# Batch 1's first transform stage cut into half steps between batch 0's column pairs, early weight decoding from one ring of buffers, twelve weight bands decoded ahead of the feed-forward part

## The chip, the cores and the metric

The kernel runs on one core of a Trainium2 chip. The metric is the device time of one launch in microseconds. Before the change the median of three runs is 2731.85 us (2729.75 to 2733.45).

## The reference

Eight batches of 3008 tokens of 256 channels go through a frequency-domain mixing and then through a gated feed-forward part; both weight matrices of the latter come in float64, and the kernel decodes them itself into two float32r words each (hi and lo).

```
X = rfft(x, axis=1);  Xr, Xi = real, imag            # x: 8 x 3008 x 256
Yr = Xr @ w_r - Xi @ w_i + b_r
Yi = Xr @ w_i + Xi @ w_r + b_i
Y  = soft_threshold(Yr, 0.01) + 1j * soft_threshold(Yi, 0.01)
y  = irfft(Y, n=3008, axis=1).reshape(24064, 256)
h  = y @ w_in                                        # w_in: 256 x 2048, float64
out = (h * clip(h + 3, 0, 6) / 6) @ w_out            # w_out: 2048 x 256, float64
```

## The kernel before

**The transform of a batch** has three parts, each a Python generator whose yields are the points at which other work may be put between its steps. `stage1(b)` (line 252) takes seven sets of rows of x; for each set it forms a sum `e` and a difference (in place in `xin`), and for each of the two (the index c) splits it into hi and lo (`xs`: a ScalarE cast and a subtraction), multiplies by the 47-point transform (three matmuls into `ps_a`), copies the product to `a` and stores it to the DRAM scratch scr1. That is fourteen steps, one yield each. For batch 0 the work is spread over VectorE and GpSimd and all inputs are loaded at once; for later batches every sum, difference and subtraction is GpSimd's, `xin`, `e`, `xs` and `a` have one buffer each, and the next set is loaded behind the second product of a set.

`middle(b)` (line 339) handles 24 columns in twelve pairs. A pair is loaded from scr1 (`bt`, with its matrix `f`), transformed (`s2`, four matmuls of line 362, split into `X`), mixed with the weights, biased and thresholded (`s3`, tile `tc`), moved across partitions by four DMAs (`zt`), split again (`s4`, tile `z`), transformed back (`s5`), copied to `pt` and stored to the DRAM scratch scr2. `segment(b, k)` (line 454) loads columns of scr2 (`qt`), runs the last 47-point transform (line 482) and adds and subtracts the halves into `raw`, the feed-forward part's input. `prepare(c)` (line 521) forms the Strassen-like differences `T` of a chunk of 512 tokens and splits them into seven `yb` operands on GpSimd.

**Decoding.** `decode` (line 169) loads a band of float64 words (`st`) and rebuilds exponent and mantissa in seven VectorE instructions (lines 184 to 192) and two ScalarE ones. `in_band` then runs six GpSimd instructions and three hi/lo splits whose subtractions are VectorE's; `out_band` runs two GpSimd multiplications. There are eight bands of each matrix. `EARLY` and `LATE` name the tiles that lend their space to `st`, `e` and `m`, `r`.

**The feed-forward part** walks over 376 units: 47 chunks of 512 tokens by 8 bands. A unit's phases a to d are seven blocks of three matmuls each into `pd`, `pb` and `pc` (with the band's `w_in`), its gate is one ScalarE activation, one VectorE multiplication and a split into `gs`, and three units later four blocks of three matmuls go into `po` (with the band's `w_out`). The first chunk needs band f at its f-th unit, so all sixteen bands must be there when the first eight units are through; the end of that pass is the first `ot` (line 604), where a chunk's `po` is scaled and sent out.

**What sets the order.** Up to the feed-forward part it is the code of lines 610 to 622: a decode, then 36 steps of batch 0's `middle` with a decode behind every fifth, then six steps of batch 1's `stage1`, then two segments of batch 0 and the first chunk's operands. Eight bands are decoded by then. From there on, `lay` (line 627) spreads generators over numbered slots, four to a unit; the rest of batch 1's `stage1` goes over the units 1 to 8, batch 1's `middle` begins at unit 9, and the other eight bands are decoded behind the units 2 to 6 (line 697). Each engine works its instructions off in order, and so does the queue of SyncE (SP), which issues every DMA; a scheduler may move an instruction of one engine past its neighbours, so the final order stands in the built program.

## Time and profile before

| | |
|---|---|
| median of three runs | 2731.85 us |
| the profiled execution | 2734.95 us |
| its span, first to last instruction | 2733.1 us |
| busy: PE, DVE, ACT, POOL | 95%, 73%, 67%, 31% of the span |
| mean granted TensorE clock | 0.976 |

The share of PE is an average: in the page's forty slices of 68.3 us PE stands at five or six tenths in the first four and at nine from the seventh on. The chain of work that ended last is PE for 68% of the span. Times below count from the first instruction of the span.

### The profile page before, as it was taken

To read this page: it belongs to the slowest core of one execution; us is meant where nothing else is said; L and a number is where in the kernel's file an instruction comes from. 1 tells how busy PE (TensorE), PEld (TensorE's weight loads), DVE (VectorE), ACT (ScalarE), POOL (GpSimd) and SP (SyncE) were. 2 spreads that over 40 slices of the span, in tenths; PEclk is the share of its full clock that TensorE was granted. 3 is DMA by queue.
4 is the path that set the end of the run, shared out by engine and by line. 5 is a ranking of instruction groups with operands and counts; after the bars stand their busy time and mean duration, and the time that the engine had idled before them with its cause. 6 is when DMAs were issued, how large, how long until landed. Compare 5 with 4: busy or idle time off the path is not lost.

```text
span 2733.1 us, 44514 instructions
## 1 busy us (share of the span) xinstructions
PE 2593.4 (95%) x16432; PEld 2317.1 (85%) x16432; DVE 1983.8 (73%) x3222; ACT 1832.4 (67%) x3591; POOL 836.6 (31%) x788
## 2 busy tenths in 40 slices
PE   5656999999999999999999999999999999999999
PEld 4544888888898898888898888988898999999997
DVE  7627877777777777777777777777777777766666
ACT  4434667766776676677767677767676667666766
POOL 3356433333322233223422343233221212122210
PEclk9876999999999999999999999999999999999999
DMA  6532442232222222222312232123221121100000
GB/s 193 159 90 68 117 123 82 82 82 80 65 68 81 74 82 67 68 75 73 90 57 72 75 96 68 57 74 95 74 67 56 58 61 49 49 23 31 16 19 16
DMA packets 150818, 200.51 MB, mean 73 GB/s; under 512 B 16975, under 2 KB 104775, under 8 KB 150599
## 3 DMA queue, kind: packets, MB, share of 16 engines
q1 hardware_dynamic: 150599, 197.65, 25.0%
q8 instruction: 129, 2.11, 0.3%
q14 instruction: 90, 0.74, 0.1%
HBM read 97.45 MB, written 74.97 MB: 63 GB/s over the span
## 4 chain that ended last, share of the span: by engine, by line
PE 68%; DVE 11%; ACT 8%; issue 6%; POOL 5%; DMA 2%; ACTq 0%; DVEq 0%; SPq 0%; POOLq 0%
PE po L136 29%; PE pb L136 15%; PE ps_a L136 9%; PE pc L136 8%; PE pd L136 4%; ACT r L581 3%; DVE r L583 3%; PE ps_a L482 2%; DVE gs L130 2%; ACT gs L129 2%; PE ps_a L362 2%; DMA xin<-in_x 2%; DVE h L546 2%; DVE X L130 1%; POOL xs L130 1%
## 5 line engine op out<-in xcount | busy, mean ns | idle before, releaser
L136 PE MATMUL po<-gs,w_out_hi 128*128 128x512 f32 x3008 | 954.3, 398 | 3.4 <-DVE gs L130 3.4
L583 DVE SCALAR_TENSOR_TENSOR r<-r,h 128x1024 f32<-128x1024 f32 x376 | 478.5, 1273 | 386.6 <-ACT r L581 386.6
L136 PEld LDWEIGHTS po<-gs,w_out_hi 128*128 128x128 f32 x3008 | 567.6, 189 | 76.3 <-DVE gs L130 4.7
L136 PE MATMUL po<-gs,w_out_lo 128*128 128x512 f32 x1504 | 609.7, 406 | 6.8 <-POOL w_out_lo L227 5.3
L136 PE MATMUL pb<-yb,w_in_hi 128*128 128x256 f32 x3008 | 604.5, 282 | 0.8 <-POOL yb L130 0.8
L130 DVE TENSOR_TENSOR gs<-r,gs 128x1024 fp32r<-128x1024 f32 x376 | 474.6, 1262 | 120.7 <-ACT gs L129 117.4
L581 ACT ACTIVATE r<-h,three 128x1024 f32<-128x1024 f32 x376 | 433.2, 1152 | 186.2 <-DVE h L546 183.6
L136 PEld LDWEIGHTS pb<-yb,w_in_hi 128*128 128x128 f32 x3008 | 465.9, 190 | 51.4 <-POOL yb L130 1.2
L129 ACT CAST gs<-r 128x1024 fp32r<-128x1024 f32 x376 | 396.0, 1053 | 130.9 <-DVE r L583 116.2
L130 POOL TENSOR_TENSOR yb<-T,yb 128x256 fp32r<-128x256 f32 x188 | 205.9, 1106 | 826.4 <-ACT yb L129 826.1
L136 PE MATMUL pb<-yb,w_in_lo 128*128 128x256 f32 x1504 | 428.1, 285 | 8.7 <-ACT p L543 4.0
L546 DVE TENSOR_TENSOR h<-pc,u 128x256 f32<-128x256 f32 x752 | 313.5, 417 | 77.7 <-PE pc L136 66.0
L543 ACT COPY u<-pb 128x256 f32<-128x256 f32 x752 | 277.4, 371 | 112.4 <-PE pb L136 106.1
L136 PEld LDWEIGHTS pb<-yb,w_in_lo 128*128 128x128 f32 x1504 | 285.6, 190 | 68.2 <-ACT p L543 8.0
L136 PE MATMUL pc<-yb,w_in_hi 128*128 128x256 f32 x1504 | 299.4, 280 | 0.5 <-POOL yb L130 0.5
L136 PEld LDWEIGHTS po<-gs,w_out_lo 128*128 128x128 f32 x1504 | 285.1, 190 | 16.6 <-POOL w_out_lo L227 5.9
L574 ACT COPY h<-pb 128x256 f32<-128x256 f32 x376 | 140.4, 373 | 142.6 <-PE pb L136 141.1
L136 PE MATMUL pc<-yb,w_in_lo 128*128 128x256 f32 x752 | 217.0, 289 | 18.3 <-DVE h L546 17.4
L136 PEld LDWEIGHTS pc<-yb,w_in_hi 128*128 128x128 f32 x1504 | 231.4, 189 | 1.6 <-POOL yb L130 0.7
L130 POOL TENSOR_TENSOR xs<-xin,xs 120x512 fp32r<-120x512 f32 (+1 forms) x52 | 69.8, 1343 | 343.1 <-ACT xs L129 293.4
L136 PEld LDWEIGHTS pc<-yb,w_in_lo 128*128 128x128 f32 x752 | 142.4, 189 | 32.9 <-DVE h L546 31.0
L546 DVE TENSOR_TENSOR h<-pd,p 128x256 f32<-128x256 f32 x376 | 156.4, 416 | 3.5 <-ACT p L543 3.0
(128 smaller groups left out, 4015.7 us busy)
## 6 DMA issues: line engine op xcount, KB each, us to landing
bt<-scr SPq DMA_DIRECT2D x96, 256.0 KB, 3.0
zt<-tc SPq DMA_DIRECT2D x384, 64.0 KB, 2.0
scr<-pt SPq DMA_DIRECT2D x96, 256.0 KB, 2.0
out<-ot SPq DMA_DIRECT2D x94, 256.0 KB, 2.0
xin<-in_x SPq DMA_DIRECT2D x48, 480.0 KB, 4.7
scr<-a SPq DMA_DIRECT2D x96, 240.0 KB, 2.5
qt<-scr SPq DMA_DIRECT2D x96, 240.0 KB, 3.4
f<-in_f SPq DMA_DIRECT2D x96, 128.0 KB, 2.9
```

The costliest lines, as they stand in the source:

```text
L129: nc.scalar.copy(out=hi, in_=src)
L130: (on or nc.vector).tensor_tensor(out=lo, in0=src, in1=hi.bitcast(F32), op=ALU.subtract)
L136: nc.tensor.matmul(out=ps, lhsT=a, rhs=b, start=start and n == 0, stop=stop and n == len(todo) - 1, skip_group_check=more,)
L362: nc.tensor.matmul(out=psv[:, dh, :, u, :], lhsT=data[:, u, dh * P : (dh + 1) * P], rhs=f[:, u, :], start=True, stop=True,)
L482: nc.tensor.matmul(out=ps[:, cs * w + g * rows : cs * w + (g + 1) * rows], lhsT=qt[:rows, cs, g, dh * P : (dh + 1) * P], rhs=f47_s[2][:row ...
L543: nc.scalar.copy(out=t, in_=ps)
L546: nc.vector.tensor_tensor(out=hs[i][:, u, half * H : (half + 1) * H], in0=ps, in1=keep.pop((i, n)), op=ALU.add)
L574: nc.scalar.copy(out=hs[i][:, 1, :H], in_=pb)
L581: nc.scalar.activation(out=r, in_=h, func=AF.Relu, bias=three, scale=1.0)
L583: nc.vector.scalar_tensor_tensor(out=r, in0=r, scalar=6.0, in1=h, op0=ALU.min, op1=ALU.mult)
```

## The change

`stage1` of the batches 1 to 7 gets a second yield per product, between the split of its operand and the matmuls, so it has 28 steps of half the size. From the eleventh of the 36 steps of batch 0's `middle`, every second one is followed by such a half step (13 in all). In front of each of the first two segments stand two decodes with the `LATE` tiles and two more half steps. So twelve bands are decoded and seventeen half steps done (eight and a half products) where there were eight bands and six products; the other eleven half steps go over the units 2 to 8, and four bands stay for the units 4 to 6.

`EARLY` now takes `e`, `m` and `r` from the nine `yb` buffers alone; the four words of `w_four` move from there to `T` and `qt`. `LATE` uses tiles of `middle` (`X`, `bt`, `tc`, `z`, `zt`, `pt`) instead of those of `stage1`, and batch 0's `pt` uses `ot` instead of `xs` and `xin`. From batch 2 on `stage1` is laid with 29 calls over the same units where it had 15.

```diff
@@ -226,8 +226,8 @@
         for t, part in zip(wout_s, (mf, rf)):
             nc.gpsimd.tensor_tensor(out=cut(t, 1), in0=part, in1=base, op=ALU.mult)
 
-    EARLY = (("raw", "yb", "yb", "yb"), ("raw", "ot", "T"), ("raw", "ot", "qt"))
-    LATE = (("xin", "bt", "tc"), ("X", "e", "xs"))
+    EARLY = (("raw", "yb", "yb", "yb"),)
+    LATE = (("X", "bt", "tc"), ("z", "bt", "zt", "pt"))
     bands = [(in_band, 0), (in_band, 1)]
     for f in range(nf):
         bands.append((out_band, f))
@@ -280,6 +280,8 @@
                 tag = ("xs", "z", "h")[q % 3 if b == 0 else 0]
                 xs = [t[:rows, :w] for t in twin([P, 2 * D], F32R, "xs", tag)]
                 split(*xs, src, nc.vector if b == 0 and (c == 0 or i % 2 == 0) else nc.gpsimd)
+                if b:
+                    yield
                 ps = room(b == 0 and c)
                 product(ps[:rows, :w], [([t[:rows, c * R47 : c * R47 + rows] for t in f47_s[:2]], xs)])
                 a = space([P, 2 * D], F32, "a", ("a", "h", "h")[q % 3] if b == 0 else "a")[:rows, :w]
@@ -324,7 +326,7 @@
             nc.sync.dma_start(out=bias_s, in_=bias)
             nc.sync.dma_start(out=sgn_s, in_=sgn)
             g64_t = loaded(g64, P, P, "g64", "ot")
-            w_four += [[space([P, 2 * D], F32R, "w", "yb") for _ in range(2)] for _ in range(2)]
+            w_four += [twin([P, 2 * D], F32R, "w", tag) for tag in ("T", "qt")]
             todo = weights()
         if i >= 8:
             next(todo, None)
@@ -428,7 +430,7 @@
         def s5(g):
             ps = room(b == 0)
             product(ps, [(g64_s, [t.rearrange("p k d -> p (k d)") for t in zs.pop(g)])])
-            pt = space([P, 2, D], F32, "pt", tag(g, "pt", "xs", "xin"))
+            pt = space([P, 2, D], F32, "pt", tag(g, "pt", "ot", "ot"))
             nc.scalar.copy(out=pt, in_=ps.rearrange("p (k d) -> p k d", d=D))
             nc.sync.dma_start(out=dst[:, 2 * g : 2 * g + 2, :], in_=pt)
 
@@ -607,17 +609,21 @@
             nc.sync.dma_start(out=out[dh * P : (dh + 1) * P, c * T : (c + 1) * T], in_=ot)
 
 
-    mid, nxt = middle(0), stage1(1)
+    mid, nxt, early = middle(0), stage1(1), 0
     decode_next(EARLY)
     for i in range(3 * (NK // 2)):
         next(mid)
         if i % 5 == 3:
             decode_next(EARLY)
+        if i >= 10 and i % 2 == 0:
+            early += 1
+            next(nxt)
     run(mid)
-    early = 6
-    for i in range(early):
-        next(nxt)
     for k in range(2):
+        for _ in range(2):
+            decode_next(LATE)
+            early += 1
+            next(nxt)
         run(segment(0, k))
     run(prepare(0))
 
@@ -647,8 +653,7 @@
         g = prepare(c)
         for n in range(8):
             slots.setdefault(max(0, 4 * (8 * c - 5) + 2 * n), []).append(g)
-    rest = 14 - early
-    lay(nxt, rest + 1, 1, 8)
+    lay(nxt, 29 - early, 2, 8)
     for b in range(B):
         for k in range(len(SEGS)):
             if (b, k) not in ((0, 0), (0, 1)):
@@ -656,7 +661,7 @@
         if b:
             lay(middle(b), 3 * (NK // 2) + 2, max(9, per * (b - 1) - 14), begin[b, 0] - 1.5)
         if b > 1:
-            lay(stage1(b), 15, max(9, per * (b - 2) - 10), per * (b - 1) - 16)
+            lay(stage1(b), 29, max(9, per * (b - 2) - 10), per * (b - 1) - 16)
 
     def fill(q):
         for g in slots.get(q, []):
```

What the new code does to the order is seen in three places. First PE, from the last column pairs of batch 0 to its first segment (`xs` products are batch 1's stage 1, `z` products the pairs' back transform, `qt` products the segments). Before, with the last two pairs and the two products of the first set just ahead of these rows:

```order
L136 MATMUL ps_a<-xs,f_lo 120x512
L136 MATMUL ps_a<-xs,f_hi 120x512 x2
L136 MATMUL ps_a<-xs,f_lo 120x512
L136 MATMUL ps_a<-xs,f_hi 120x512 x2
L136 MATMUL ps_a<-xs,f_lo 120x512
L136 MATMUL ps_a<-xs,f_hi 120x512 x2
L136 MATMUL ps_a<-xs,f_lo 120x512
L482 MATMUL ps_a<-f_all,qt 128x120
L136 MATMUL ps_a<-xs,f_hi 120x512 x2
L482 MATMUL ps_a<-f_all,qt 128x120 x7
L136 MATMUL pd<-yb,w_in_lo 128x256
```

and with the change:

```order
L136 MATMUL pb<-z,g_lo 128x512
L136 MATMUL pb<-z,g_hi 128x512 x2
L136 MATMUL ps_a<-xs,f_lo 120x512
L136 MATMUL ps_a<-xs,f_hi 120x512 x2
L136 MATMUL pb<-z,g_lo 128x512
L136 MATMUL pb<-z,g_hi 128x512 x2
L136 MATMUL pb<-z,g_lo 128x512
L136 MATMUL pb<-z,g_hi 128x512 x2
L484 MATMUL ps_a<-f_all,qt 128x120 x8
L136 MATMUL ps_a<-xs,f_lo 120x512
L136 MATMUL ps_a<-xs,f_hi 120x512 x2
L484 MATMUL ps_a<-f_all,qt 128x120 x8
```

Before, all six products stand between the last pair and the first segment. With the change the products stand between the pairs, and only one, behind the first segment, is left in that place.

Second DVE, from the last pair's `z` on (`raw` is written by the segments, `h` is the feed-forward part's). Before:

```order
L130 TENSOR_TENSOR w_in_lo<-m,w_in_hi 128x256
L130 TENSOR_TENSOR w_in_lo<-m,w_in_hi 128x128
L130 TENSOR_TENSOR w_in_lo<-e,w_in_hi 128x512
L130 TENSOR_TENSOR z<-zt,z 128x512
L492 TENSOR_TENSOR raw<-ps_a,odd 128x240
L504 TENSOR_TENSOR raw<-ps_a,odd 128x230
L492 TENSOR_TENSOR raw<-ps_a,odd 128x240
L504 TENSOR_TENSOR raw<-ps_a,odd 128x230
L492 TENSOR_TENSOR raw<-ps_a,odd 128x42
L492 TENSOR_TENSOR raw<-ps_a,odd 128x198
L504 TENSOR_TENSOR raw<-ps_a,odd 128x230
```

and with the change, where the last `z` is 16 rows above the first of these:

```order
L191 TENSOR_SCALAR m<-st 128x512
L187 SCALAR_TENSOR_TENSOR e<-st,e 128x512
L192 SCALAR_TENSOR_TENSOR m<-st,m 128x512
L184 TENSOR_SCALAR e<-st 128x512
L189 TENSOR_SCALAR m<-st 128x512
L185 TENSOR_SCALAR e<-e 128x512
L191 TENSOR_SCALAR r<-st 128x512
L186 TENSOR_SCALAR e<-e 128x512
L192 SCALAR_TENSOR_TENSOR r<-st,r 128x512
L494 TENSOR_TENSOR raw<-ps_a,odd 128x240
L506 TENSOR_TENSOR raw<-ps_a,odd 128x230
L187 SCALAR_TENSOR_TENSOR e<-st,e 128x512
```

Between the last `z` and the first `raw` there was nothing; now the end of one `w_out` band, all of a `w_in` band and a `w_out` band, and six of the seven decoding instructions of a further `w_in` band stand there, 24 rows.

Third DVE in the first pass of the feed-forward part. Before, about the fifth unit's gate:

```order
L184 TENSOR_SCALAR e<-st 128x512
L189 TENSOR_SCALAR m<-st 128x512
L185 TENSOR_SCALAR e<-e 128x512
L191 TENSOR_SCALAR m<-st 128x512
L186 TENSOR_SCALAR e<-e 128x512
L192 SCALAR_TENSOR_TENSOR m<-st,m 128x512
L187 SCALAR_TENSOR_TENSOR e<-st,e 128x512
L130 TENSOR_TENSOR w_in_lo<-m,w_in_hi 128x256
L130 TENSOR_TENSOR gs<-r,gs 128x1024
L130 TENSOR_TENSOR w_in_lo<-m,w_in_hi 128x128
L130 TENSOR_TENSOR w_in_lo<-e,w_in_hi 128x512
```

and with the change, about the gate of the second unit:

```order
L130 TENSOR_TENSOR gs<-r,gs 128x1024
L548 TENSOR_TENSOR h<-pd,p_1562 128x256
L585 SCALAR_TENSOR_TENSOR r<-r,h 128x1024
L548 TENSOR_TENSOR h<-pc,u_1594 128x256
L130 TENSOR_TENSOR w_in_lo<-m,w_in_hi 128x256
L130 TENSOR_TENSOR w_in_lo<-m,w_in_hi 128x128
L130 TENSOR_TENSOR w_in_lo<-e,w_in_hi 128x512
L548 TENSOR_TENSOR h<-pc,u_1538 128x256
L130 TENSOR_TENSOR gs<-r,gs 128x1024
L191 TENSOR_SCALAR m<-st 128x512
L585 SCALAR_TENSOR_TENSOR r<-r,h 128x1024
```

Before, three `w_in` bands have their `w_in_lo` subtractions in such a place, ahead of or between the gates; with the change one band has, and it is these rows.

## Rows read from the trace of the kernel before

**Rows 1.** Busy time of each engine by stage; the clock is the granted TensorE clock.
```profile
core 0: us, PE busy (x) PEld busy (x) DVE busy (x) ACT busy (x) POOL busy (x), PEclk, DMA share, GB/s
40.00:128.00 88.00, 63.37 (x419) 57.12 (x420) 68.17 (x124) 39.81 (x77) 30.40 (x34) 0.87 0.54 160
128.00:172.00 44.00, 15.65 (x41) 8.60 (x40) 1.43 (x4) 8.50 (x18) 17.86 (x17) 0.54 0.35 94
172.00:200.00 28.00, 22.05 (x122) 18.82 (x122) 13.87 (x29) 15.47 (x35) 18.65 (x21) 0.89 0.36 92
200.00:298.00 98.00, 67.13 (x305) 55.35 (x304) 71.17 (x113) 47.77 (x97) 60.09 (x52) 0.74 0.30 82
300.00:400.00 100.00, 98.02 (x643) 88.77 (x644) 79.77 (x124) 70.15 (x140) 34.49 (x28) 1.00 0.42 119
```

**Rows 2.** PE's waits between 128 and 172 us: total, times, longest.
```profile
PE ps_a L136 <- ACT xs L129: 20.2, 6, 6.8
```

**Rows 3.** Timeline of POOL, batch 1's stage 1: start, duration, instruction, idle before.
```profile
142.97 1.26 POOL L276 TENSOR_TENSOR e<-xin 120x512 f32<-120x512 f32 x1 [4.13 <-DMA xin<-in_x]
149.32 1.27 POOL L130 TENSOR_TENSOR xs<-xin,xs 120x512 fp32r<-120x512 f32 x1 [2.52 <-ACT xs L129]
154.72 1.26 POOL L276 TENSOR_TENSOR e<-xin 120x512 f32<-120x512 f32 x1 [4.13 <-DMA xin<-in_x]
```

**Rows 4.** Timeline of SP, the first segment's load.
```profile
131.90 0.89 SPq L463 DMA_DIRECT2D qt<-scr  x2
```

**Rows 5.** Timeline of DVE, from the last pair to the second segment.
```profile
126.80 0.69 DVE L130 TENSOR_TENSOR z<-zt,z 128x512 fp32r<-128x512 f32 x1
165.28 0.41 DVE L492 TENSOR_TENSOR raw<-ps_a,odd 128x240 f32<-128x240 f32 x1 [37.80 <-ACT odd L490]
177.34 0.39 DVE L504 TENSOR_TENSOR raw<-ps_a,odd 128x230 f32<-128x230 f32 x1
```

**Rows 6.** DVE between 40 and 128 us, line 411, by lines: count, busy, mean ns.
```profile
L411 DVE TENSOR_SCALAR tc<-tc 128x512 f32<-128x512 f32 x12 | 7.9, 657 | 0.1
```

**Rows 7.** Timeline of DVE, line 411 once with POOL idle.
```profile
116.52 0.41 DVE L411 TENSOR_SCALAR tc<-tc 128x512 f32<-128x512 f32 x1
```

**Rows 8.** Timeline of DVE and POOL, one early w_in band from start to end.
```profile
95.64 0.43 DVE L184 TENSOR_SCALAR e<-st 128x512 int32<-128x512 int32 x1 [2.54 <-DMA st<-in_w_in]
97.93 0.68 DVE L187 SCALAR_TENSOR_TENSOR e<-st,e 128x512 int32<-128x512 int32 x1
...
98.75 1.27 POOL L203 TENSOR_TENSOR m<-m 128x512 f32<-128x512 f32 x1 [13.17 <-ACT m L193]
103.48 0.52 POOL L213 TENSOR_TENSOR e<-m,e 128x128 f32<-128x128 f32 x1
...
104.68 0.69 DVE L130 TENSOR_TENSOR w_in_lo<-e,w_in_hi 128x512 fp32r<-128x512 f32 x1 [1.00 <-ACT w_in_hi L129]
```

**Rows 9.** Timeline of POOL, the first chunk's operands.
```profile
177.30 0.74 POOL L526 TENSOR_TENSOR T<-raw,T 128x256 f32<-128x256 f32 x1 [0.60 <-DVE raw L492]
182.12 0.73 POOL L130 TENSOR_TENSOR yb<-raw,yb 128x256 fp32r<-128x256 f32 x1
```

**Rows 10.** PE's waits between 200 and 290 us.
```profile
PE pd L136 <- DVE w_in_lo L130: 8.4, 2, 5.3
PE po L136 <- POOL w_out_lo L227: 5.3, 2, 3.5
```

**Rows 11.** DVE's waits between 200 and 300 us.
```profile
DVE h L546 <- PE pc L136: 12.1, 6, 5.6
DVE w_in_lo L130 <- ACT w_in_hi L129: 7.1, 4, 2.9
```

**Rows 12.** Timeline of DVE, the first finished chunk.
```profile
298.37 0.69 DVE L604 TENSOR_SCALAR ot<-po 128x512 f32<-128x512 f32 x1
```

**Rows 13.** The chain that ended last, three pieces: start, length, what.
```profile
291.82 0.35 PE pb L136 x3
292.54 0.70 PE po L136 x3
293.35 1.44 PE ps_a L136 x12
```

**Rows 14.** PE's stage 1 products, second and third matmul, by lines: busy, mean, idle before.
```profile
L136 PE MATMUL ps_a<-xs,f_hi 120*120 120x512 f32 (+1 forms) x210 | 69.6, 413 | 11.1 <-POOL xs L130 9.8 <-DVE xs L130 1.2
```

**Rows 15.** PE's waits between 128 and 300 us.
```profile
PE ps_a L136 <- POOL xs L130: 9.8, 11, 2.1
```

## The prediction

> **What bounds the kernel now.** I read the busy time by stage first, because the page's 95% for PE is an average [rows 1]. From 300 us on PE is the bound: 98.02 of 100 us busy at the full clock of 2.4 GHz (granted clock 1.00). Nothing in the change gives that part less PE work, so what can be won lies ahead of 300 us. There the stages have other limits. From 40 to 128 us (batch 0's column pairs beside the early decoding) DVE is the busiest with 68.17 of 88 us and PE has 63.37. From 128 to 172 PE has 15.65 of 44 us at a clock of 0.54, and DVE 1.43: nobody is busy. From 200 to 298 PE has 67.13 of 98 us at a clock of 0.74.
>
> The waits of PE tell what the empty stage is [rows 2]: 20.2 us for ScalarE's `xs`, batch 1's stage 1. POOL's timeline shows its chain [rows 3]: a set starts at 142.97, the next at 154.72, so 11.75 us for two products, each link (load, sum, cast, subtraction, product, store) waiting for the one before. Batch 0's first segment doesn't depend on it. Its load was issued at 131.90 [rows 4], but its matmuls stand in PE's queue behind the six products, so DVE, which ended the last pair's `z` at 127.5, gets to `raw` at 165.28 after 37.80 us of idleness [rows 5].
>
> In the first pass of the feed-forward part the waits are another kind: PE for `w_in_lo` (8.4 us) and `w_out_lo` (5.3) [rows 10], DVE for PE (12.1) and for the cast of a band (7.1) [rows 11]. The bands come late, and DVE, which decodes them, stands in its own queue between the gates of the units.
>
> **The change, part by part.**
>
> *Half steps between the pairs.* Thirteen half steps put sixteen POOL instructions, some 8 us of ScalarE and six products of three matmuls into a stage where POOL has 30.40 of 88 us [rows 1]. DVE gets no instruction more. What it may lose is time beside POOL: line 411 takes 0.41 us alone [rows 7] and 657 ns in the mean of the twelve in this stage [rows 6], 12 x 0.25 = 3.0 us lost beside the 34 POOL instructions of [rows 1]. Sixteen more would cost this line 1.4 us; for the other lines I double it and take 3 us. The bounds are nothing, and sixteen times a whole instruction of 1.27 us [rows 3], 20 us; I stay near the measured row. Below nothing the port gives no way, since no instruction leaves the stage. The new ring of `EARLY` leaves `st` its two buffers, so the bands' loads go out as before; I cost it at nothing, with one such load wait, 2.54 us [rows 8], as a loss or a gain. The three single-buffer tiles of stage 1 are waited for by POOL and SP there. On SP an input load waits for POOL's last use of `xin`, with the pairs' `zt` and `pt` transfers behind it. By the order each such load comes after that use was due, so I cost it at nothing; if that cover fails, a pair is late by the set's link, and that is in the 20 us.
>
> The Trainium skill, page "SBUF — State Buffer", section "Who interferes with whom", says that VectorE and GpSimd share a port pair that whoever comes first holds for its whole instruction, while the other fully blocks. By that rule taken at its strictest the stage would grow by the 20 us of the upper bound and not by 3. The trace agrees that the lock exists (657 against 410 ns), not that each POOL instruction meets one.
>
> *From the last pair to the first operands.* The last `z` then ends at 127.5 + 3 = 130.5. The six products no longer stand ahead of the segment (in PE's order one product is left, behind it). What is late next is DVE, with 24 decoding instructions ahead of `raw`. I price them by one early band [rows 8]: seven instructions from 95.64 to 98.61, so 3.0 us, and from the first to the end of `w_in_lo` at 105.37 9.7 us, POOL's six taking 98.75 to 104.0 of it. So: the end of the first `w_out` band 0.6 (131.1); a whole `w_in` band 9.7, plus 2.6 because POOL first has two multiplications and two instructions of stage 1 (4 x 1.27 from 131.7 to 136.8, where the band could start at 134.2), to 143.4; the six instructions left of the next `w_out` band 2.6 (146.0); six of the following `w_in` band 2.4. `raw` starts at 148.4 where it started at 165.28, 17 us earlier. The segment's load stands on SP behind loads that wait for the first of these bands to leave `st`, at about 134; that leaves 14 us until it is needed, where it had 33. From the first `raw` to the end of the second segment's it took 12.5 us [rows 5]; I take the same, with the rest of that band in it: 160.9. Then `T` and `yb` took until 182.85 [rows 9], 5.1 us behind the segment's end at 177.73; two multiplications of a `w_out` band now stand between, 2.6. The first chunk is ready at about 169 instead of 183: 14 us.
>
> *The first pass of the feed-forward part.* Before it runs from 182.85 to the first `ot` at 298.37 [rows 12], 115.5 us. PE's own work in it, by the intervals of the chain at full clock (0.35 us for three matmuls of a block, 0.70 for three of `po`, 1.44 for twelve mixing ones) [rows 13]: 32 `po` blocks are 22.4 us; eleven units of seven blocks 27.0; less four blocks done early 1.4; stage 1, two segments and about two of batch 1's pairs some 12. Together 60 us. Half of the 115.5 us was thus waiting or a halved clock. With twelve bands ready, one `w_in` and two `w_out` bands are left to decode in the pass, and one such wait on DVE instead of three (last excerpts of the order). DVE had 71.17 us of work from 200 to 298 us [rows 1], with seven to eight bands in it; a band is 3.0 us there and half as much again for the subtractions, so five fewer leave some 50, less than PE's 60. So PE should bound the pass, at a rate between 79% (172 to 200 us, the part of the pass with hardly any decoding) and 98% [rows 1]. I take 88%: 68 us, and the first `ot` at 169 + 68 = 237 instead of 298: **61 us**. In parts: 17 us at the first segment (the 3 us of the pairs are taken off already), 3 of them given back ahead of the first operands, 47 more in the pass.
>
> *Batches 2 to 7.* Fourteen calls more of `stage1` per batch, over some 40 units, move no work. PE never waited for POOL's `xs` behind 300 us: the whole kernel's 9.8 us [rows 14] are those of the stretch to 300 [rows 15]. I cost it at nothing; the upper bound is a rival.
>
> *The sum.* The profiled execution took 2734.95 us for a span of 2733.1; 2734.95 - 61 = 2674. The median of the runs shown is 3.1 us below that execution, so 2671.
>
> **The rivals.**
>
> *The first pass keeps its pace.* If the 10.5 us per unit were the start-up of the gates and the low clock, not the bands, only the earlier start stays: 14 us, 2718. For it: the clock was 0.74 in the whole pass, and 60 us of work at 1.2 GHz are 120. Against it: between 172 and 200 us, with the bands at hand, the clock was 0.89 and PE busy 79% [rows 1], and the waits that are named are those for bands. The skill's page "TensorE: Matmul & The Clock Gate", section "What's actually happening", holds that the throttled state is the default and activity releases it; by that rule the clock follows the gaps and is no cause of its own. The trace agrees: 0.54 in the emptiest stage, 1.00 in the fullest.
>
> *The pairs are stretched.* If a product in PE's queue waits for POOL while POOL works off a band (98.75 to 104.0, 5.25 us [rows 8]), six products cost up to 31 us instead of 3: 61 - 28 = 33 us gained, 2699. For it: POOL waits in its queue for ScalarE's band casts (13.17 us ahead of one). Against: the half step puts the matmuls two pair steps behind their operands.
>
> *Slower: the half steps make PE wait in the part that it bounds.* Place: the 84 products of batches 2 to 7. Price: up to one POOL instruction of 1.27 us each, 107 us, which makes 2671 + 107 = 2778. It decides from 61 / 84 = 0.73 us per product. For it: operands and matmuls now sit in slots of their own, with one `xs` buffer. Against: no such wait is seen today, and the operand comes earlier, not later.
>
> **How the numbers follow.** The forecast gets 0.73, with its own range from 2659 (pairs not stretched, pass at 98%: 10 us better, and 2 for the runs' spread) to 2696 (pairs stretched by 20 us, pass at 79%: 25 us worse). The stretched pairs get 0.09, the pace kept 0.11, the slower case 0.04, and 0.03 goes to small losses that eat the whole gain. What a measurement of this kernel can tell is about 0.2%, 5.5 us. So faster 0.93, within 0.03, slower 0.04. The range for 8 in 10 goes from 2654 to 2706: it takes in the forecast's own and the stretched pairs, and leaves out the kept pace and the slower case.
>
> **What the changed profile would show.** The last `z` between 127 and 134 us; `raw` at 145 to 152 with no idleness of DVE beyond some 4 us at a time ahead of it; the first chunk's last `yb` at 165 to 172; the first `ot` at 228 to 247; the clock at 0.9 or more from 172 to 230; no waits of PE for `w_in_lo`. The forecast is wrong if the pairs end behind 150 us, if PE waits for `w_out_lo` or DVE for the band casts in the pass for over 10 us in all, or if PE's waits for `xs` reappear behind 300 us.

## The result and the profile after

The changed kernel takes 2701.83 us (median of four runs, 2700.22 to 2705.12), the kernel before beside it 2730.8 us (2728.49 to 2733.45): a ratio of 0.9895, 95% interval 0.9878 to 0.9912. It is faster by 29 us; 61 were forecast. The time lies inside the range, but more than half of the expected gain is missing.

Busy time by stage, as in [rows 1]:

```profile
core 0: us, PE busy (x) PEld busy (x) DVE busy (x) ACT busy (x) POOL busy (x), PEclk, DMA share, GB/s
40.00:128.00 88.00, 67.12 (x421) 61.85 (x422) 67.00 (x110) 39.16 (x77) 40.71 (x41) 0.83 0.57 166
128.00:172.00 44.00, 14.27 (x50) 10.23 (x50) 30.42 (x52) 15.60 (x31) 28.58 (x25) 0.62 0.60 166
172.00:200.00 28.00, 20.45 (x98) 17.39 (x97) 22.81 (x42) 16.07 (x39) 21.15 (x25) 0.62 0.37 104
200.00:298.00 98.00, 87.36 (x529) 76.85 (x529) 75.16 (x110) 62.01 (x124) 45.86 (x40) 0.95 0.29 81
300.00:400.00 100.00, 96.84 (x637) 87.06 (x636) 79.82 (x127) 70.35 (x144) 41.99 (x37) 1.00 0.40 114
```

From 200 us on it went the way that was forecast: the clock 0.95 for 0.74, PE busy 87 of 98 us for 67. But the stage from 128 to 172 us, out of which most of the products were taken, is as empty for PE as before (14.27 us; what fills it now is DVE's decoding, 30.42 us for 1.43), and from 172 to 200 us the clock is 0.62 where it was 0.89. Five instants say how far each step got. DVE's timeline (start, duration, instruction), to be read against [rows 5, 12]:

```profile
146.73 0.69 DVE L130 TENSOR_TENSOR z<-zt,z 128x512 fp32r<-128x512 f32 x1
...
166.31 0.40 DVE L494 TENSOR_TENSOR raw<-ps_a,odd 128x240 f32<-128x240 f32 x1
...
181.28 0.38 DVE L506 TENSOR_TENSOR raw<-ps_a,odd 128x230 f32<-128x230 f32 x1
...
268.78 0.68 DVE L606 TENSOR_SCALAR ot<-po 128x512 f32<-128x512 f32 x1
```

and POOL's, the first chunk's last operands [rows 9]:

```profile
189.42 2.10 POOL L130 TENSOR_TENSOR yb<-raw,yb 128x256 fp32r<-128x256 f32 x3
```

The row holds three subtractions of 0.7 us: the first chunk's last one and two of the second chunk's. So the first chunk is ready at 190.1 us. Expectations below that speak of 191.5 us, and the first-chunk times that go with it, count the second chunk's two as well; the text counts the first chunk's seven operands in every run, as [rows 9] do.

| instant | before | forecast | after |
|---|---|---|---|
| last `z` of the pairs | 126.8 | 130 | 146.7 |
| first `raw` | 165.3 | 148.4 | 166.3 |
| second segment's end | 177.7 | 160.9 | 181.7 |
| first chunk's operands | 182.9 | 169 | 190.1 |
| first `ot` on DVE | 298.4 | 237 | 268.8 |

The pairs end 20 us later than before, the first chunk 7 us later, and all of the gain is made in the pass behind it, the stretch up to the first `ot`: 79 us instead of 115.5. The last `ot` starts at 2696.19 instead of 2729.28 us, 33.1 us earlier, so what stood at the first output (29.6 us on DVE, 33.7 us at ScalarE's `ot`, the chunk's other half) is kept to the end. That these two executions lie 33 us apart and the medians 29 is the profiled execution of before, 4.2 us above the median of the runs beside the change.

### The profile page after: what moved, and what is told of

It is laid out like the page before. It is cut to its first block, busy times and chain, and to the rows that moved or that the text cites. A ratio compares the mean times of both kernels' runs of the same rounds, so it can differ in the third digit from the quotient of the medians.

```text
span 2700.0 us, 44497 instructions
## 1 busy us (share of the span) xinstructions
PE 2585.8 (96%) x16432; PEld 2315.4 (86%) x16432; DVE 1993.3 (74%) x3222; ACT 1826.4 (68%) x3591; POOL 827.6 (31%) x788
## 4 chain that ended last, share of the span: by engine, by line
PE 73%; DVE 9%; ACT 8%; issue 5%; POOL 3%; DMA 2%; SPq 0%; ACTq 0%; DVEq 0%; POOLq 0%
PE po L136 30%; PE pb L136 16%; PE ps_a L136 9%; PE pc L136 9%; PE pd L136 4%; PE ps_a L484 3%; ACT r L583 2%; ACT gs L129 2%; PE ps_a L364 2%; DVE gs L130 2%; DVE r L585 2%; DVE h L548 1%; DMA xin<-in_x 1%; DVE X L130 1%; DVE tc L414 1%
## 5 line engine op out<-in xcount | busy, mean ns | idle before, releaser
L130 DVE TENSOR_TENSOR gs<-r,gs 128x1024 fp32r<-128x1024 f32 x376 | 480.5, 1278 | 127.7 <-ACT gs L129 124.3
L136 PEld LDWEIGHTS pc<-yb,w_in_lo 128*128 128x128 f32 x752 | 142.2, 189 | 33.4 <-DVE h L548 31.9
```

Of the source, the lines that this page charges most:

```text
L130: (on or nc.vector).tensor_tensor(out=lo, in0=src, in1=hi.bitcast(F32), op=ALU.subtract)
L136: nc.tensor.matmul(out=ps, lhsT=a, rhs=b, start=start and n == 0, stop=stop and n == len(todo) - 1, skip_group_check=more,)
```

## The experiments

Each was run once beside a run of the kernel before (the last two four times); where a total differs from the changed kernel's by 5 us or less I read nothing into it, since the changed kernel's own runs span 4.9 us. The instants are of each run's own trace. In the changed kernel and the three runs whose code differs from it only in the loop behind the pairs, the last `z` starts between 145.1 and 146.7 us, so an instant is good to about 2 us. A line of three dots in a diff stands for lines left out. Batch 1's stage 1 is called "the stage" here.

### What stretches the pairs

**No half steps there.**
```diff
-        if i >= 10 and i % 2 == 0:
-            early += 1
-            next(nxt)
...
-    lay(nxt, 29 - early, 2, 8)
+    two = (next(nxt, None) for _ in nxt)
+    lay(two, 13, 1, 8)
```


> The thirteen half steps of batch 1's stage 1 are taken out from between the pairs; they run as whole steps in the first units. All buffers and the twelve bands stay as in the changed kernel. In the changed kernel the last z of the pairs ended at 146.7 us, in the kernel before at 126.8. If the half steps stretch the pairs, by whatever way, the last z ends at 126 to 130. If the new buffers (one ring for the early bands, other places for pt and w_four) stretch them, it stays at 144 to 148. The span follows only in part, since six more products stand in the first units: 2685 to 2705 by the first theory, 2700 to 2715 by the second.

The last `z` at 134.3, total 2715.58 us. So 12.4 of the 20 us come from the half steps, 7.5 from something else. The first chunk was ready 15 us earlier, and yet the kernel is 14 us slower than the changed one: the stage's products now stand in the pass, where PE waited 17.8 us for `xs`. So the place of the half steps pays, even at a price that the forecast had too low.

**Products with ready operands.**
```diff
+            w_ready = [t[:rows, :w] for t in w_m] if b == 1 else None
...
-                product(ps[:rows, :w], [([t[:rows, c * R47 : c * R47 + rows] for t in f47_s[:2]], xs)])
+                product(ps[:rows, :w], [([t[:rows, c * R47 : c * R47 + rows] for t in f47_s[:2]], w_ready if b == 1 and q < 6 else xs)])
```


> The first six products of batch 1's stage 1 read a constant that has long been ready in place of their operand; sums, casts, subtractions, copies, stores and loads are all still issued at the same places (batch 1's output then isn't the reference's). Theory of the queue's head: the products' waits at the head of TensorE's queue in the changed kernel (2.42 + 1.44, 5.63 + 0.74, 4.86 + 1.14 = 16.2 us) go, and the last z ends at 130 to 134, the span at 2683 to 2690. Theory of the port (GpSimd's sixteen more instructions hold VectorE up) and theory of SyncE's queue (stores and loads of stage 1 ahead of the pairs' own transfers): nothing that they name is gone, the last z stays at 143 to 147, the span at 2697 to 2703.

PE's waits from 60 to 147 us (total, times, longest), the changed kernel, then this run:

```profile
PE ps_a L136 <- ACT xs L129: 12.9, 3, 5.6
PE ps_a L136 <- POOL xs L130: 3.3, 3, 1.4
```
```profile
PE ps_a L136 <- ACT xs L129: 1.6, 1, 1.6
PE ps_a L136 <- POOL xs L130: 1.4, 1, 1.4
```

13 us of waiting are gone, and the last `z` is at 146.27: nothing gained (2704.88 us). One thing blurs the test: this run's pairs start 6 us later (the first `pt` at 72.25 us instead of 66.12), for a reason that I don't know. But by the seventh pair the two are level (`pt` at 107.45 and 107.27), and behind it, where the two longest waits were (5.6 and 4.9 us), they take the same time. So TensorE's queue, my first theory and the one in the prediction's rival, falls: PE's wait there held nothing else up.

**Whole steps** (the product right behind its operand).
```diff
-        if i >= 10 and i % 2 == 0:
-            early += 1
-            next(nxt)
+        if i >= 10 and i % 4 == 0:
+            for _ in range(1 if i == 32 else 2):
+                early += 1
+                next(nxt)
```


> Between the pairs the steps are whole: the product stands right behind its operand's sum, cast and subtraction, where the changed kernel put two pair steps between them. The number of instructions, their engines and the last place are the same. Theory of the queue's head: each of the six products now waits for its whole link, 3.5 to 6 us instead of 2.7 in the mean, so the last z moves from 146.7 to 151 to 166 and the span to 2707 to 2722. Theory of the port: the same instructions beside VectorE, 145 to 149, span 2698 to 2705. Theory of SyncE's queue: the same stores, 143 to 149.

The last `z` at 142.95, 3.8 us earlier, not later (2705.88 us). It speaks against TensorE's queue once more.

**Stores from ScalarE's queue.**
```diff
-                nc.sync.dma_start(out=dst, in_=a.rearrange(...))
+                (nc.scalar if b == 1 and q < 6 else nc.sync).dma_start(out=dst, in_=a.rearrange(...))
```


> The six stores of batch 1's first products are issued from ScalarE's queue instead of SyncE's. In the changed kernel SyncE stood 11.2 us in three such stores, waiting for ScalarE's copy, with zt and pt transfers behind them. Theory of SyncE's queue: the last z ends at 136 to 142. Theories of GpSimd's work and of the load: 145 to 150, since ScalarE gets six issues more.

The last `z` at 148.73, 2706.41 us: SyncE's stores are not it.

**Earlier load.**
```diff
                 split(*xs, src, ...)
+                if c and b and i + 1 < len(sets):
+                    shapes.append(load(i + 1))
                 if b:
                     yield
...
-                if c and b and i + 1 < len(sets):
-                    shapes.append(load(i + 1))
```


> The next set's input load is issued half a step earlier, right behind the last subtraction that reads xin, not behind the product and its store. Theory of the queue's head: two of the three product pairs waited because this load landed late (GpSimd's sum waited 4.38 and 6.20 us for it), so some 8 to 10 us of the 16.2 go: the last z at 136 to 140, the span 2690 to 2696. Theory of SyncE's queue: a load that waits for GpSimd now stands earlier in the queue with zt, pt and the bands' loads behind it; the last z stays at 145 or goes to 150. Theory of the port: 146, no change.

The last `z` at 144.99, 2703.89 us. The pairs up to the ninth came 9 us earlier (`pt` copied at 116.92 instead of 126.00) and lost it again at the tenth (132.41 against 130.34). The shift of one load moved the place of the wait.

**No GpSimd work, no loads, neither.** Three runs. The stage's first four sets without GpSimd's sums and subtractions (the sum and the difference of a set now stand under `if not bare`):
```diff
+            bare = b == 1 and i < 4
+            if not bare:
...
-            for c, src in enumerate((e, plus)):
+            for c, src in enumerate((minus, plus) if bare else (e, plus)):
...
+                if bare:
+                    nc.scalar.copy(out=xs[0], in_=src)
+                    xs[1] = w_m[1][:rows, :w]
+                else:
+                    split(*xs, src, ...)
```


> In the first four sets of batch 1's stage 1 GpSimd's four instructions per set are left out: ScalarE casts the loaded rows themselves, and the low part is a constant (batch 1's output then isn't the reference's). Loads, casts, products, copies and stores stay. The run with ready operands left the pairs' end at 146.3, so TensorE's queue is not it; left are GpSimd and the queues of ScalarE and SyncE. Theory of GpSimd's work (it delays the bands' own GpSimd work, and holds VectorE at the port: VectorE's pairs and bands cost some 6 us more in the changed kernel than before): the last z ends at 131 to 137, near the 134.3 without any half step. Theory of the load (ScalarE's cast waits at the head of its queue until the set's input has landed, and tc, z and pt of the pairs wait behind it): the casts still wait for the same loads, the last z at 141 to 147.

without their loads:
```diff
+            if b != 1 or i >= 4:
                 nc.sync.dma_start(out=xins[i][:rows, :, :w], in_=src)
...
+            to = plus
+            if b == 1 and i < 4:
+                plus = minus = bias_s[:rows, :w]
...
```


> The first four sets of batch 1's stage 1 load nothing: GpSimd's sums read a constant that is ready, and everything behind them is issued as in the changed kernel (batch 1's output then isn't the reference's). Theory of the load: GpSimd's waits for it (4.38 and 6.20 us and what lies behind them on ScalarE) go, the last z ends at 134 to 139. Theory of GpSimd's work: all its instructions are still there, the last z at 143 to 147. Theory of SyncE's queue: four issues of 0.4 us less, 144 to 147.

and without both (the first edit, with a constant for the loaded rows, and no load):
```diff
+            for c, src in enumerate([bias_s[:rows, :w]] * 2 if bare else (e, plus)):
```


> The first four sets of batch 1's stage 1 neither load anything nor use GpSimd: ScalarE casts a constant, the low part is a constant; products, copies and stores stay (batch 1's output then isn't the reference's). Alone, leaving out GpSimd's work ended the pairs at 138.9 us and leaving out the loads at 141.4, against 146.7 with both and 134.3 without any half step between the pairs. If the two are separate prices, they add up and the last z ends at 132 to 135; if they are one chain seen at two places, it ends at 137 to 140, and the rest is the products, casts and copies themselves. The first output 11 to 20 us earlier than 268.8.

DVE's last `z` in the three:

```profile
138.85 0.69 DVE L130 TENSOR_TENSOR z<-zt,z 128x512 fp32r<-128x512 f32 x1
```
```profile
141.38 1.36 DVE L130 TENSOR_TENSOR z<-zt,z 128x512 fp32r<-128x512 f32 x1 [0.65 <-ACT z L129]
```
```profile
135.96 0.69 DVE L130 TENSOR_TENSOR z<-zt,z 128x512 fp32r<-128x512 f32 x1
```

7.9, 5.4 and 10.8 us earlier; totals 2697.45, 2692.28 and 2685.77 us. So both are causes, and together they are more than half of the 19.9 us. The third run lies between its two expectations; the overlap of 2.5 us is hardly above what an instant is good for. (These runs take them out of the four half steps beside the late bands too, so they can't be subtracted from the 12.4 us of the first run.) What DVE loses beside GpSimd is seen by comparing equal work: busy time from 40 us to the end of the pairs, with the same 131 instructions of DVE, the changed kernel and the run without GpSimd's 16 instructions:

```profile
40.00:148.00 108.00, 73.87 (x440) 65.98 (x441) 78.16 (x131) 46.84 (x92) 51.88 (x52) 0.80 0.57 164
```
```profile
40.00:139.00 99.00, 71.79 (x439) 63.17 (x439) 71.60 (x131) 45.70 (x92) 32.18 (x36) 0.83 0.62 177
```

DVE is busy 6.6 us less. That is one reading and no fixed price: without both, DVE is busy 75.91 us for 132 instructions (40 to 136.6 us), 2 us less than in the changed kernel, and without any half step 73.97 us for 132 (40 to 135 us), 4 us less. The loads' part is a wait that travels from queue to queue; POOL's for them from 40 to 148 us:

```profile
POOL e L276 <- DMA xin<-in_x: 13.2, 3, 6.2
```

The changed kernel's timelines of POOL, ACT and DVE at the end of the pairs:

```profile
133.13 1.26 POOL L276 TENSOR_TENSOR e<-xin 120x512 f32<-120x512 f32 x1 [6.20 <-DMA xin<-in_x]
...
136.92 1.72 POOL L203 TENSOR_TENSOR m<-m,r 128x512 f32<-128x512 f32 x1
```
```profile
134.42 0.62 ACT L129 CAST xs<-e 120x512 fp32r<-120x512 f32 x1 [3.52 <-POOL e L276]
...
135.48 0.49 ACT L417 ACTIVATE tc<-tc,sgn 128x256 f32<-128x256 f32 x1
135.88 0.60 ACT L129 CAST z<-zt 128x512 fp32r<-128x512 f32 x1
...
143.51 0.62 ACT L129 CAST w_in_hi<-e 128x512 fp32r<-128x512 f32 x1 [2.88 <-POOL e L213]
144.04 0.58 ACT L434 COPY pt<-pb 128x512 f32<-128x512 f32 x1
...
146.10 0.60 ACT L129 CAST z<-zt 128x512 fp32r<-128x512 f32 x1
```
```profile
132.16 0.68 DVE L414 TENSOR_TENSOR tc<-tc 128x512 f32<-128x512 f32 x1
136.51 1.00 DVE L130 TENSOR_TENSOR z<-zt,z 128x512 fp32r<-128x512 f32 x1 [3.68 <-ACT z L129]
```

POOL waits 6.20 us for a load; ACT's cast of `xs` waits for POOL's sum; the last pair's `tc` was ready at 132.84 and is taken at 135.48, the `z` of the pair before it behind that, and DVE waits 3.68 us. The band's `m`, behind three of the stage's instructions on POOL, starts at 136.92, and `pt` at 144.04 stands on ACT behind the cast of that band. So does the last pair's `z`: its transfers had landed by 138.5 us, and its cast starts at 146.10. The Trainium skill, page "PSUM — Partial Sum Buffer", section "Engine vs sequencer instructions", calls the queues of ScalarE, VectorE and GpSimd strictly first in, first out; these rows agree.

**The cast on GpSimd.**
```diff
+                if b == 1 and i < 4:
+                    nc.gpsimd.tensor_copy(out=xs[0], in_=src)
+                    nc.gpsimd.tensor_tensor(out=xs[1], in0=src, in1=xs[0].bitcast(F32), op=ALU.subtract)
```


> In the first four sets of batch 1's stage 1 the cast of the operand is done by GpSimd instead of ScalarE; loads, sums, subtractions, products, copies and stores as in the changed kernel. GpSimd gets two instructions more per set. Theory of ScalarE's queue (its casts wait for GpSimd's sum and so for the load, with the pairs' tc, z and pt behind them): the last z ends at 138 to 143. Theory of GpSimd's work (its bands come late and it holds VectorE at the port): 148 to 152.

The last `z` at 149.73, 2708.02 us. Taking the wait off ScalarE's queue gains nothing if GpSimd gets more to do.

**Three parts and the earlier load.**
```diff
+            if b == 1 and i < 3:
+                yield
             for c, src in enumerate((e, plus)):
...
+                if c and b and i + 1 < len(sets):
+                    shapes.append(load(i + 1))
...
-    lay(nxt, 29 - early, 2, 8)
+    lay(nxt, 32 - early, 1, 8)
```


> Batch 1's first three sets are put in three parts instead of two: GpSimd's two sums in a step of their own, the cast and its subtraction a step later, the product and store a third step later; and the next set's load is issued right behind the last subtraction. Five products stand between the pairs instead of six, none of the work is left out. Theory of the load and of ScalarE's queue (a cast that waits for GpSimd's sum, and so for the load, holds up tc, z and pt behind it): the cast's operand is there when its turn comes, the last z at 137 to 142 as without loads (141.4), the first output at 254 to 262, the span at 2690 to 2697. Theory of GpSimd's work: all its instructions are still beside VectorE and ahead of the bands', the last z at 144 to 148, the span at 2698 to 2704.

The last `z` at 142.2, just outside the 137 to 142 of the load's theory, but 2710.82 us: one product less stands between the pairs, and PE waited 12.9 us for `xs` behind 150 us.

The 7.5 us without half steps stay in part open. Two of them are there from the first `pt` on (66.15 against 64.21), while other runs with the same code up to there show 65.0 to 66.4. The rest falls on the last two pairs: there the run without half steps has on POOL a sum of the stage ahead of the band that the last `z` stands behind, and the sum waits and is slow:

```profile
121.56 4.63 POOL L276 TENSOR_TENSOR e<-xin 120x512 f32<-120x512 f32 x1 [4.94 <-DMA xin<-in_x]
126.27 1.26 POOL L277 TENSOR_TENSOR xin<-xin 120x512 f32<-120x512 f32 x1
127.49 1.26 POOL L203 TENSOR_TENSOR m<-m,r 128x512 f32<-128x512 f32 x1
```

It is one of the four half steps called with the late bands, which the scheduler put that far ahead. I didn't test it by itself. The late bands themselves may be a part too: in the square below the last `z` is 2.0 us later than before with their new tiles alone (128.79), and 3.0 us earlier than in the changed kernel with the old ones (143.70), both hardly above what an instant is good for.

What is left without GpSimd's work and the loads, 9.2 us more than before, is there by the tenth pair (its `zt` lands 7.9 us later than before). That run's ACT, at the ninth pair:

```profile
113.36 0.62 ACT L129 CAST w_in_hi<-e 128x512 fp32r<-128x512 f32 x1 [1.66 <-POOL e L213]
113.89 0.61 ACT L129 CAST z<-zt 128x512 fp32r<-128x512 f32 x1
```

The ninth pair's `zt` had landed at 106.9 us, and its cast waits 7 us behind the casts of a weight band, which wait for POOL's part of the band; in the kernel before the same cast starts 0.1 us behind the landing. So the half steps also change where a band's casts stand among the pairs' on ACT. This is read from the traces; no run moves those casts by themselves.

### What the pass and the first chunk depend on

**Segment's load first, ten bands, eight bands.** Three edits of the same loop.
```diff
+        seg = segment(0, k)
+        next(seg)
         for _ in range(2):
             decode_next(LATE)
```


> The load of each of the first two segments is issued ahead of the two bands that stand before the segment, not behind them. In the changed kernel SyncE issued it at 156.56 behind two band loads that wait for VectorE, and TensorE waited up to 13.0 us for it; the first raw started at 166.3, 18.9 us behind the last z's end. If that place costs the time, the first raw starts at 156 to 160, the last yb of the first chunk ends 6 to 9 us earlier than 191.5, the first output moves from 268.8 to 260 to 264 and the span from 2700 to 2692 to 2696. If VectorE's 24 decoding instructions bound it, raw stays at 163 to 166 and the span at 2698 to 2703. The pairs' end is not touched: 146.

```diff
-        for _ in range(2):
-            decode_next(LATE)
+        decode_next(LATE)
+        for _ in range(2):
             early += 1
             next(nxt)
```


> One band instead of two stands ahead of each of the first two segments; the two bands left are decoded in the units 3 and 4. Theory of VectorE's decoding ahead of raw (24 instructions and their waits, 18.9 us from the last z's end to the first raw): the first raw starts 8 to 10 us earlier, at 156 to 158, the first chunk's last yb ends at 178 to 184, the pairs' end stays at 146. By the prediction's own step each band in the pass costs it: two more bands give back 4 to 10 us, first output 262 to 270, span 2694 to 2702. If the bands in the pass cost nothing as long as they come in time, first output at 256 to 261, span 2688 to 2693.

```diff
         for _ in range(2):
-            decode_next(LATE)
             early += 1
             next(nxt)
```


> The four bands ahead of the first two segments are left out there and decoded in the units, as in the kernel before: eight bands ahead, the half steps and the buffers as in the changed kernel. This is the half steps' part alone. By the prediction's third step (12 bands ahead take the pass from 115.5 us to 68) the pass is long again: first raw at 150 to 156, last yb of the first chunk at 172 to 178, the pass at 95 to 115 us, first output at 270 to 290, span 2703 to 2722, and TensorE waits for w_in_lo and w_out_lo again. If the bands ahead are not what shortens the pass, but the products taken out of its way, the pass stays at 70 to 82 us, the first output at 245 to 258, span 2680 to 2690.

First `raw` at 164.3, 164.7 and 161.9, totals 2701.85, 2703.32 and 2700.78 us: all the same within the runs' spread. The last seemed to refute the prediction's third step. But its trace shows that the edits did not do what they say: with eight bands called ahead, 13 bands had passed DVE's line 187 by 179.5 us (180.6 in the changed kernel). And with the segment's load first in the code, SP still issued it at 154.46 (156.56 in the changed kernel), behind a band's load. A further run has three edits at once: no band called ahead, the segment's load first, and the earlier load of the stage. It was expected to bring the first `raw` at 152 to 157 us if the segment's load bound it, and at 160 to 165 if DVE's decoding did. It came at 160.72, right behind a band's line 187 and with DVE busy up to it, though PE waited 7.6 us for the load; 2701.70 us, the same again. In all these runs the scheduler took a band about as early as in the changed kernel, wherever the code called it. So the question became which edit frees the tiles.

**The square.** The kernel before with the new tiles of `LATE` alone, and the changed kernel with the old ones and no band called ahead. (The second keeps the rest of the change too: the ring of `EARLY`, the places of `pt` and `w_four`, the 29 calls per batch. "Half steps alone" below stands for all of that.)
```diff
-    LATE = (("xin", "bt", "tc"), ("X", "e", "xs"))
+    LATE = (("X", "bt", "tc"), ("z", "bt", "zt", "pt"))
```


> The kernel before with one line changed: the late bands are decoded in X, bt, tc and z, bt, zt, pt instead of xin, bt, tc and X, e, xs, so they share no tile with batch 1's stage 1 any more. No half steps, eight bands ahead in the code. Theory that the tiles held the bands back: the bands are decoded during the empty stage from 128 to 165 us by themselves, the pass shrinks from 115 us to 80 to 95, the first output moves from 298.4 to 262 to 282, the span from 2733 to 2700 to 2718. Theory that the half steps (products out of the way) or the extra calls shorten it: first output 292 to 300, span 2728 to 2735.

```diff
-    LATE = (("X", "bt", "tc"), ("z", "bt", "zt", "pt"))
+    LATE = (("xin", "bt", "tc"), ("X", "e", "xs"))
...
-            decode_next(LATE)
```


> Half steps, EARLY, pt and w_four as in the changed kernel, but the late bands in the old tiles, which they share with batch 1's stage 1, and none called ahead of the segments. Theory that the tiles held the bands back: the bands come late again, TensorE waits for w_in_lo and w_out_lo, the pass takes 95 to 115 us, the first output at 270 to 295, span 2702 to 2728. Theory that the half steps shorten the pass: pass 75 to 82 us, first output 250 to 264, span 2685 to 2698.

| | first `raw` | first chunk | first `ot` | pass | span |
|---|---|---|---|---|---|
| before | 165.3 | 182.9 | 298.4 | 115.5 | 2733.1 |
| new tiles alone | 188.7 | 206.3 | 282.9 | 76.6 | 2715.2 |
| half steps alone | 155.8 | 171.1 | 281.4 | 110.3 | 2718.8 |
| both (changed) | 166.3 | 190.1 | 268.8 | 78.6 | 2700.0 |

The two halves give 17.9 and 14.3 us, together 32.2 of the 33.1 measured. The tiles bring the bands ahead (without a call for it all sixteen have passed DVE's line 187 by 182 us; in the kernel before the ninth does at 200) and shorten the pass by 32 to 39 us, and they cost the first chunk 19 to 23 us. The half steps bring the first chunk 12 to 16 us forward and change the pass by -5 and +2. PE's waits in the pass, half steps alone (171 to 282 us), which are those of [rows 10]:

```profile
PE pd L136 <- DVE w_in_lo L130: 9.7, 3, 4.2
PE po L136 <- POOL w_out_lo L227: 2.6, 1, 2.6
```

In the changed kernel neither is left. What the bands cost ahead of the first chunk is seen on SP: the segment's load with the old tiles, and in the changed kernel:

```profile
149.48 8.44 SPq L465 DMA_DIRECT2D qt<-scr  x4
```
```profile
155.22 0.59 SPq L173 DMA_DIRECT2D st<-in_w_in  x1
...
156.56 1.00 SPq L465 DMA_DIRECT2D qt<-scr  x2
```

**One band at a time.** No band called ahead, one set of tiles for all late bands; then the same with whole steps.
```diff
-    LATE = (("X", "bt", "tc"), ("z", "bt", "zt", "pt"))
+    LATE = (("X", "bt", "tc"),)
...
-            decode_next(LATE)
```


> The changed kernel with no band called ahead of the first two segments and one set of tiles (X, bt, tc) for all late bands, so that they can run ahead only one behind the other. By the square of runs (tiles: 17.9 us, half steps: 14.3, both: 33.1) the bands ahead shorten the pass by some 35 us and delay the first chunk by some 20. Theory that fewer bands at a time give the chunk back without losing the pass: first raw 156 to 160, first chunk 176 to 182, pass 77 to 82, first output 254 to 263, 2687 to 2696. Theory that what the chunk gains the pass loses: first output 264 to 272, 2697 to 2705.

> As the run with one set of tiles for the late bands, and with whole steps between the pairs (product right behind its operand), which alone ended the pairs 3.8 us earlier. Theory that fewer bands at a time give the chunk back: first output 250 to 260, 2684 to 2694. Theory that the pass loses it: 262 to 270, 2696 to 2704.

The first chunk came at 176.8 us, 13 earlier, the first `ot` at 263.5, 5 earlier, and the total is the same: 2703.79 us, ratio 0.9895 (0.9879 to 0.9912). Its last `ot`:

```profile
2697.89 0.69 DVE L606 TENSOR_SCALAR ot<-po 128x512 f32<-128x512 f32 x1 [2.70 <-PE po L136]
```

From the first to the last `ot` it took 2434.4 us, the changed kernel 2427.4, and PE was busy 2408.3 us of it instead of 2404.3: an early first output is worth less where PE has left other work for later. That accounts for 4 of the 7 us; the other 3 I can't assign. With whole steps 2708.43 us, ratio 0.991 (0.9895 to 0.9925). No version that does all of the work beats the changed kernel.

## Why the prediction was wrong

The order of the instants in the table gives the size of each step's error; they add up to 31.8 us at the first `ot`. None of the prediction's own signs of being wrong came (the pairs ended at 147.4, not behind 150), so those were set too wide.

**The step that failed is the first, "half steps between the pairs", priced at 3 us.** It measured 19.9, 17 us of the error. I had priced DVE's time beside POOL (3 us forecast; 2 to 7 measured, by the run that it is compared with) and put the waits at nothing, because each load "comes after that use was due". The loads did land late (POOL waited 13.2 us for `xin` from 40 to 148 us), and the wait was passed on: to ACT by the order of its queue, to the bands by POOL's. The 20 us of the prediction's upper bound was met in size, and in its mechanism only where it adds that a failed cover would be in it; it had been counted as sixteen blocked DVE instructions, and leaving all of POOL's work out gives back 7.9. Of the 19.9, POOL's work and the loads are 10.8; the other 9.1 no run assigns, and the traces show a part of them as casts of the pairs that stand behind a band's on ACT. The rival "the pairs are stretched" named 2699 us, close to what came, but by luck: it put 28 us more at the pairs and nothing behind them, where 17 and 15 came, and its mechanism, the product at the head of PE's queue, is refuted by the run with ready operands.

**From the last pair to the first operands.** From the last `z`'s end to `raw` it took 18.9 us (17.9 forecast), the bands priced rightly. SP's 14 us of slack were not there, by PE's waits from 130 to 180 us:

```profile
PE ps_a L484 <- DMA qt<-scr: 14.9, 2, 13.0
```

From `raw` to the chunk it took 23.8 us instead of 20.6; the next bands stood between the segments on DVE and among the `T` on POOL. 4 us of the error together.

**The first pass.** The mechanism was right, the square shows it: with the bands ahead, PE's waits for them are gone, though it was the tiles and not the calls that brought them. The changed kernel by stage:

```profile
147.00:166.00 19.00, 5.56 (x19) 4.10 (x19) 14.80 (x25) 6.76 (x13) 12.56 (x11) 0.50 0.58 161
190.15:268.80 78.65, 68.67 (x406) 60.25 (x405) 58.30 (x91) 51.68 (x103) 42.39 (x40) 0.92 0.31 85
240.00:269.00 29.00, 28.71 (x198) 25.89 (x197) 22.30 (x39) 20.99 (x45) 10.44 (x13) 1.00 0.38 108
```

PE was busy 68.7 of the 78.6 us, 87% where I had taken 88%; the term that was too small is the work, 69 us where I had counted 60. The clock of 0.92 instead of 1.00 is a part of that; how much of it, I didn't separate. 11 us of the error. The rival "pace kept" did not come: the clock was 0.50 (the level of 1.2 GHz) from 147 to 166 us with PE busy 5.56 of 19 us, and 1.00 from 240 to 269 us with PE busy 28.71 of 29. The page "TensorE: Matmul & The Clock Gate" of the Trainium skill, section "What's actually happening", holds that the throttled state is the default and activity releases it; these rows agree.

**Batches 2 to 7.** Right: no wait of PE for `xs` behind 300 us, and 33.1 us at the last `ot` where ScalarE's first one came 33.7 us earlier (263.34 instead of 297.04). The half steps' extra calls cost nothing that the trace shows.

## What to carry to other kernels

Work that is a chain of latencies (load, sum, cast, subtract, product, store) isn't priced by its busy time when it is put between the steps of another such chain: in queues that keep their order each of its links can hold up the other chain on every engine it touches. Give such a chain a bound from the waits of its links as the trace of before shows them. Here that is 4.13 us for each of the four loads [rows 3], 16.5 us where the forecast had nothing; it is a bound and not a price, since leaving the loads out gave back 5.4. And when a scheduler orders the work, ask which tile holds an instruction back: a change of buffers can move more than a change of calls, and an experiment that only moves a call may change nothing. The trace of an experiment says whether the edit did what it was meant to do.

## What was not expected of the hardware

VectorE is not the only one that pays where the two work side by side. In the run without half steps POOL's sum over 120 x 512 starts at 121.56 us and takes 4.63 us (the row above) where it takes 1.26 elsewhere. DVE's rows beside it, the first and the last of eight that stand there without a gap:

```profile
121.51 0.41 DVE L184 TENSOR_SCALAR e<-st 128x512 int32<-128x512 int32 x1
...
124.39 0.68 DVE L187 SCALAR_TENSOR_TENSOR e<-st,e 128x512 int32<-128x512 int32 x1
```

None of the eight takes longer than elsewhere (0.41 and 0.68 us), and the sum ends 1.1 us behind the last of them, about its own length. It is one row, and POOL's spans in a profile are rough. The Trainium skill, page "SBUF — State Buffer", section "Who interferes with whom", says that whoever comes first holds the shared port pair and the other blocks; this row agrees for POOL, as [rows 6] and [rows 7] do for DVE.
